# FNet mixing followed by a sigmoid GLU on one Trainium2 core: batch 1's row copies, table loads and folds moved to earlier steps

## The chip, the cores and the metric

The kernel runs on one core of a Trainium2 chip, in float32 throughout. The metric is the device time of one execution in microseconds (us), the median of the runs shown. The core has five engines with a queue of instructions each: PE (matmuls; PEld is its weight loading), DVE (vector), ACT (scalar), POOL (GpSimd) and SP (sync, which here only issues DMAs). An engine takes its instructions in program order. The data of a DMA are moved by 16 DMA engines that all issuers share.

## The reference

```python
X = np.fft.fft(x, axis=1)                  # x: (8, 3008, 256) float32
X = np.fft.fft(X, axis=2)
x = X.real.astype(np.float32).reshape(8 * 3008, 256)
gate = 1.0 / (1.0 + np.exp(-(x @ w_gate))) # (256, 1536)
val = x @ w_val                            # (256, 1536)
out = (gate * val) @ w_out                 # (1536, 256)
```

## The kernel before

**Mathematics.** The DFT over the 256 features is folded into the gate and value weights once, at the start: `merge` (L410) multiplies each block of weights by the table `dt` and leaves the cosine and sine forms in `G1` and `G2` and one row of them, by DMA, in `ge`. The DFT over the 3008 positions is done per batch. The rows of a batch are brought into an order in which symmetric rows stand beside each other, added and subtracted ("folded"), and multiplied on PE by small tables of cosines and sines. The results are `pk` and `qk`, one column per pair of output rows k and 3008 - k. One feature column (number 128) goes its own way: `x8` holds it for batches 1 to 7, `e_joint` (L731) transforms it, the row `er` is stored to `ed` in DRAM and comes back, broadcast over the partitions, as `ek`.

**Steps.** The main loop (L1143) runs over 576 steps: 8 batches, 6 chunks of at most 252 columns, 12 blocks of 128 hidden features. A batch is 72 steps (`per`), a chunk 12 (`i0`). Step i forms the gate and value sums of block i in a PSUM bank: `seed` (ACT, L767) writes `ek` times `ge` into it, `front_a` adds the part of `pk` and `front_b` that of `qk` (PE). `gate_a` and `gate_b` (ACT and DVE) turn the two output rows of each pair into gated values `h`, a step later. `back(p, part)` (L852) multiplies them by `w_out` five steps later: three blocks form group p, and step i runs `back((i - 5) // 3, (i - 5) % 3)`. From group 4 on this takes 15 products instead of 18, for which POOL prepares sums: seven (`H_SUMS[1]`) after the group's second block and six (`H_SUMS[2]`) after its third, into the tile `sf` (L819). The products of part 1 read h5, sum 13, h8, sum 11 and sum 12, in this order; sum 11 is finished by the first of the six. At a chunk's end, `finish` (L893) spreads further sums on DVE, transposes into the tile `os` and 16 stores from SP over the next steps. `os` and `er` share one buffer (pool `op`, one buffer).

**The order of the work is written by hand.** `at(i, f)` puts f at the end of step i, `gap` into the middle of `gate_b`, `spare` ahead of `gate_b`. An engine sees the instructions in exactly this order. SP does not wait for steps: it issues as soon as the waits of each DMA allow. DMAs use eight completion semaphores in turn ("lanes", of ACT's DMAs too), and a DMA waits until the one eight before it has landed.

What batch 1 needs in its preparation, with the steps of before:

- weights: `weight_load` for jobs 13 to 17 at steps 4 to 8 (512 KB each, into the buffer `x4`, which batch 1's rows take later); two tiny `ge` DMAs per merge (L420)
- `quarter_x(1)` (L150): 23 DMAs that copy batch 1's rows within DRAM, from the input into `xr` in the needed order: three small ones of zeros, two of 384 KB (L168), 18 of 124 or 128 KB (L163); at steps 9 to 14
- `load_x(1)` (L143): `xr` into SBUF, two DMAs of 1536 KB; step 14
- `table_rows` (L203): six copies of 188 KB within DRAM, into `rtab`; step 15
- `raw_tables` (step 17) and `quarter_load` (L241, steps 18 and 19): 16 loads of 141 KB into the tile `st`; `quarter_small`, `quarter_other` and `small_ops` then form a few columns of ratios from them; `ratios[6]` is the reciprocal of L278
- `e_load` (L682): the 128th column of batches 1 to 7, seven DMAs of single floats, steps 23 to 29; `e_fold` (four POOL sums) at step 38; `e_joint` at step 40
- `fold_ops(1, 2)` (L485): 24 operations on the rows: eight additions over the feature mirror on POOL (L496, L492), six `across` sums (L505; five on DVE, one on POOL), six `feat` (L499 to L502) and four half sums (L531) on POOL; steps 21 to 51
- `e_rows(i)` (L749): loads `ek` of a chunk; the one of step 36 is issued by ACT, all others by SP

Of the kernel before, what the change touches and what calls it, by code (L numbers as in the profile page):

```python
# [81 lines left out]
def kernel(  # L82
# [10 lines left out]
    nc = tc.nc  # L93
    B, _, _, _, D = xf.shape
    F = moe_w_gate.shape[1]
    P = 128
# [5 lines left out]
    NFT = F // P  # L102
# [40 lines left out]
    def load_x(b):  # L143
        X[b] = xp.tile([P, 4, NQ, D], F32, name="x4", tag="x4")
        for h in range(0, 4, 2) if b else ():
            nc.sync.dma_start(out=X[b][:, h : h + 2], in_=XR[b][:, h : h + 2])
# [3 lines left out]
    def quarter_x(b):  # L150

        copy = nc.sync.dma_start
        src = xf[b]
        dst = XR[b] = dram.tile([P, 4, NQ, D], F32, name=f"xr{b}")
        ops = [lambda: copy(out=dst[TB : TB + 1, :, N3], in_=zero[0:1].to_broadcast([1, 4, D]))]
        for q in (1, 1 + N3):
            ops.append(lambda q=q: copy(out=dst[HP - 1 : HP, :, q], in_=zero[0:1].to_broadcast([1, 4, D])))

        def run(lo, q, t, step, skip=0, less=0):
            n = TB - skip - less  # L160
            p0 = t // NQ + step * skip
            rows = src[p0 : p0 + n] if step > 0 else src[p0 - n + 1 : p0 + 1]
            copy(out=dst[lo + skip : lo + skip + n, :, q].rearrange("p h d -> h p d"),  # L163
                 in_=rows[:, :, t % NQ].rearrange("p h d -> h p d")[:, ::step])

        for par in range(2):
            lo = par * HP
            ops.append(lambda par=par, lo=lo: copy(out=dst[lo : lo + TB, :, 0:N3], in_=src[0:TB, :, par:NQ:2]))  # L168
            for q in range(N3):
                own = 2 * q + par  # L170
                less = int((par, q) == (0, 1))
                first = int((par, q) == (0, 0))
                ops += [lambda a=a: run(*a) for a in (
                    (lo, N3 + q, M // 2 - own, -1), (lo + TB, q, M // 4 - own, -1, 0, less),
                    (lo + TB, N3 + q, M // 4 + own, 1, first, less))]
        return ops
# [12 lines left out]
    ed = dram.tile([B, NK + 1], F32, name="ed")  # L189
# [13 lines left out]
    def table_rows(par, q):  # L203

        p0, qq = divmod(M // 4 - 2 * q - par, NQ)
        nc.sync.dma_start(
            out=rtab[par * TB : (par + 1) * TB, :, q].rearrange("p t k -> t p k"),
            in_=stab[p0 - TB + 1 : p0 + 1, :, qq].rearrange("p t k -> t p k")[:, ::-1])
# [29 lines left out]
    def quarter_src(g, par, t, cols):  # L238
        return (stab[0:TB, t, par:NQ:2, cols], rtab[par * TB : (par + 1) * TB, t, :, cols])[g]

    def quarter_load(t, par):  # L241


        for name, cols in (("odd", slice(NE, NE + NO)), ("ev", slice(0, NE))):
            for g, own, lo in TILES:
                if own == par:
                    nc.sync.dma_start(out=TAB[name][lo : lo + TB, t ^ g, :, 0 : cols.stop - cols.start],
                                      in_=quarter_src(g, par, t, cols))

    def quarter_small(which, part):  # L250

        for g, par, lo in TILES:
            at_ = slice(lo, lo + TB)
            if (g, par) == (which, part):
                nc.scalar.copy(TAB["self"][at_, 0:N3], TAB["ev"][at_, g, :, 0])
                nc.scalar.copy(TAB["angle"][at_].rearrange("p (t q) -> p t q", t=2),
                               TAB["odd"][at_, :, :, 0] if g == 0 else TAB["odd"][at_, ::-1, :, 0])
# [6 lines left out]
    def small_ops():  # L264

        vec, sign = nc.vector, TAB["sign"]

        def signs():
            for g, par, lo in TILES:
                nc.gpsimd.memset(sign[lo : lo + TB], (1.0, -1.0)[g])  # L270
        return signs, (
            lambda: vec.reciprocal(TAB["less"], TAB["cos"]),
            lambda: vec.tensor_tensor(TAB["tan"], TAB["sin"], TAB["less"], op=ALU.mult),
            lambda: vec.tensor_scalar(out=TAB["less"], in0=TAB["tan"], scalar1=-1.0, scalar2=None, op0=ALU.mult),
            lambda: vec.reciprocal(TAB["self"], TAB["self"]),
            lambda: vec.tensor_tensor(TAB["other"], TAB["other"], TAB["self"], op=ALU.mult),
            lambda: vec.tensor_scalar(out=TAB["other"], in0=TAB["other"], scalar1=sign, scalar2=None, op0=ALU.mult),
            lambda: vec.reciprocal(TAB["cy"], TAB["ev"][:, 0, :, 1]),  # L278
            lambda: vec.tensor_tensor(TAB["cx"], TAB["ev"][:, 1, :, 1], TAB["cy"], op=ALU.mult),
            lambda: vec.tensor_scalar(out=TAB["cx"], in0=TAB["cx"], scalar1=sign, scalar2=None, op0=ALU.mult),  # L280
            lambda: vec.tensor_scalar(out=TAB["cy"], in0=TAB["cx"], scalar1=-1.0, scalar2=None, op0=ALU.mult))
# [391 lines left out]
    def seq_start(b):  # L673
        PQE[b] = [pqp.tile([P, NK + 1], F32, name=name, tag=name) for name in ("pk", "qk")]
        for t in PQE[b]:
            nc.vector.memset(t[:, NK:], 0.0)
# [5 lines left out]
    def e_load(b):  # L682
        nc.sync.dma_start(out=x8[:, b - 1], in_=xf[b, :, :, :, HD : HD + 1])
# [57 lines left out]
    H, SF, EK = {}, {}, {}  # L741
# [7 lines left out]
    def e_rows(i):  # L749

        b, c, _ = groups[i // 3]
        k0, n = chunks[c]
        EK[i // NFT] = ekp.tile([P, CH], F32, name="ek", tag="ek")[:, 0:n]
        queue = nc.scalar if i == 3 * NFT else nc.sync
        queue.dma_start(out=EK[i // NFT], in_=ed[b : b + 1, k0 : k0 + n].to_broadcast([P, n]))

    PF, AP, Z = {}, {}, {}
    N1 = 5
# [240 lines left out]
    sin[1][1]()()  # L999
    weight_join(3)  # L1000
    e_rows(0)

    per = NFT * len(chunks)
    side, mid, gap, spare = {}, {}, {}, {}

    def at(i, *fs):
        side.setdefault(i, []).extend(fs)
# [18 lines left out]
    i0 = NFT  # L1026
    count = 3 * len(groups)
    calm = lambda lo: (i for i in range(lo, count) if 3 <= i % i0 <= 7)
    for i, f in enumerate(quarter_x(1)):
        at(i0 - 3 + i // 4, f)  # L1030
    at(i0 + 2, lambda: load_x(1))
    for b in range(1, B):
        at(22 + b, lambda b=b: e_load(b))
    at(3 * i0 + 2, e_fold)
    later_e = []
    at(3 * i0 + 4, lambda: later_e.extend(e_joint()))
    at(3 * i0 + 5, lambda: later_e[0]())
# [1 line left out]
    at(3 * i0 + 6, made_tables)  # L1039
    at(3 * i0 + 8, lambda: later_e[2]())  # L1040
    for i in range(i0, count, i0):
        if i == 3 * i0:
            spare[i - 11] = [lambda: e_rows(3 * i0)]
        else:
            at(i - (8 if i == i0 else 11), lambda i=i: e_rows(i))

    for i in range(NQ):
        at(15, lambda i=i: table_rows(i % 2, i // 2))
    at(17, raw_tables)
    for i in range(4):  # L1050
        at(18 + i // 2, lambda i=i: quarter_load(i // 2, i % 2))
    signs, ratios = small_ops()
    at(i0, signs)
    for i in range(4):
        spare.setdefault(34 + i // 2, []).append(lambda i=i: quarter_small(i // 2, i % 2))
    at(36, quarter_other)
    for i, f in zip((36, 36, 37, 42, 43, 44, 34, 35, 51, 52), ratios, strict=True):
        gap.setdefault(i, []).append(f)

    def first_folds():  # L1060

        slots = [21, 21, 21, 22, 22, 23, 24, 25, 25, 26, 27, 27, 28, 28, 30, 33, 36, 38, 40, 42, 44, 46, 48, 51]
        for i, f in zip(slots, fold_ops(1, 2), strict=True):
            at(i, f)
        for i, f in enumerate(TURN.pop(1)):
            if i in (1, 4):
                at((38, 40)[i // 4], f)
            else:
                gap[(38, 0, 39, 40, 0, 41)[i]] = [f]
        swaps, last, first = MORE.pop(1)  # L1070
        at(41, swaps[1])
        at(52, swaps[0])
        for i, f in enumerate(first):
            gap.setdefault(45 + i, []).append(f)
        for i, f in enumerate(last):
            gap[56 + i] = [f]

    def first_ends():
        one, two = quarter_ends(1, 1), quarter_ends(1, 0)
        for i, f in zip((55, 65, 65, 66, 66, 67, 67, 68, 68, 69, 69, 70, 70, 71, 71, 72, 73, 74, 75, 76),  # L1080
                        one[0] + two[0] + one[1] + two[1], strict=True):
            gap.setdefault(i, []).append(f)
    at(19, first_folds)
    at(3 * i0 + 14, lambda: seq_start(1))
    for blk in range(2):
        mid[(5 - blk) * i0 + 5] = lambda blk=blk: quarter(1, blk)
# [56 lines left out]
    for i in range(count):  # L1143
# [13 lines left out]
        n = 3 if i >= count - 8 else 2 + (i % 2 and i not in (3 * i0 + 7, 3 * i0 + 9))  # L1157
# [80 lines left out]
```

## Time and profile before

| | |
|---|---|
| median of 3 runs (lowest to highest) | 1918.88 us (1918.55 to 1919.31) |
| the profiled execution | 1919.43 us |
| its span, first to last instruction | 1917.6 us |
| PE busy | 1900.3 us, 99% |
| DVE, ACT, POOL busy | 80%, 71%, 81% |
| granted PE clock, mean | 0.998 |
| chain of work that ended last: PE | 93% |
| queue 1 of the DMAs | 195752 packets, 106.37 MB |

A step can be found in the trace by the start of its `pf<-qk` matmuls:

| step | 8 | 16 | 21 | 26 | 31 | 35 | 36 | 40 | 41 | 42 | 43 |
|---|---|---|---|---|---|---|---|---|---|---|---|
| us | 76.24 | 103.36 | 118.98 | 134.61 | 152.27 | 164.77 | 169.36 | 181.86 | 187.40 | 194.18 | 200.17 |

How to read it: "idle before" and "waits" name what an engine waited for; SPq is the queue of SP's DMA issues. The chain of work is followed back from the last instruction. In a table by stretches, each line has the length, each engine's busy time with its number of instructions, the granted PE clock (1.00 is full), the mean busy share of the 16 DMA engines and GB/s. A timeline line has start, duration, engine, line of the kernel, operation, and out<-in.

### The profile page before, as it was taken

Reading aid. Unit: us, or ns where it says so; the run is one execution under the profiler, and the core shown is the slowest. Engines: PE = TensorE matmul, PEld = TensorE weight load, DVE = VectorE, ACT = ScalarE, POOL = GpSimd, SP = SyncE. Lnnn points to the kernel's source line nnn. Section 1 sums busy time; section 2 is a strip of 40 time slices with the busy share of each in tenths; the row PEclk is TensorE's granted clock in tenths of the full one; section 3 lists DMA queues with packets and bytes.
Section 4 is the critical chain, followed back from the end, with each engine's and each line's share of the span. In section 5 each row is a group of like instructions: output and inputs, shape, how many; then the busy total and the mean of one; then the engine's idle time right before and its main releaser. Section 6 shows DMA issues by size and latency. Waiting matters only on the chain.

```text
span 1917.6 us, 36046 instructions
## 1 busy us (share of the span) xinstructions
PE 1900.3 (99%) x11836; PEld 1758.3 (92%) x11836; DVE 1526.9 (80%) x3368; ACT 1353.5 (71%) x3235; POOL 1545.6 (81%) x2733
## 2 busy tenths in 40 slices
PE   8999999999999999999999999999999999999999
PEld 5788899999999999999999999999999999999998
DVE  7677888787978789797788877888788887977775
ACT  4876777777677777777777777677777777777775
POOL 2488879986999779997799877999789986877770
PEclk9999999999999999999999999999999999999999
DMA  8336331212022121221212112112120110010001
GB/s 313 96 124 77 89 105 44 66 46 81 15 52 72 31 80 24 63 52 32 87 36 57 42 37 86 39 47 51 33 80 15 34 41 15 15 23 19 15 18 30
DMA packets 196661, 109.33 MB, mean 57 GB/s; under 512 B 134791, under 2 KB 187762, under 8 KB 194682
## 3 DMA queue, kind: packets, MB, share of 16 engines
q1 hardware_dynamic: 195752, 106.37, 20.9%
q8 instruction: 95, 1.56, 0.4%
q14 instruction: 92, 0.75, 0.1%
q10 hardware_dynamic: 690, 0.64, 0.1%
q0 software_dynamic: 32, 0.00, 0.0%
HBM read 71.24 MB, written 47.87 MB: 62 GB/s over the span
## 4 chain that ended last, share of the span: by engine, by line
PE 93%; DMA 2%; DVE 1%; POOL 1%; ACT 1%; SPq 1%; issue 0%; DVEq 0%; ACTq 0%; POOLq 0%
PE pf L133 49%; PE po L133 41%; PE sum L133 2%; DMA x<-in_xf_dram 1%; POOL sf L819 1%; DMA rtab<-in_stab_dram 1%; PE ps L133 1%; DMA st<-rtab 1%; DMA raw<-in_moe_w_val_dram 0%; DVE z L797 0%; PE ev L133 0%; SPq L926 0%; PE od L133 0%; POOL x L505 0%; ACT pf L767 0%
## 5 line engine op out<-in xcount | busy, mean ns | idle before, releaser
L819 POOL TENSOR_TENSOR sf<-h,sf 128x168 f32<-128x168 f32 (+1 forms) x1104 | 619.6, 581 | 78.9 <-DVE h L813 76.9
L819 POOL TENSOR_TENSOR sf<-h 128x168 f32<-128x168 f32 (+1 forms) x920 | 521.7, 586 | 167.4 <-DVE h L813 166.3
L133 PE MATMUL pf<-qk,G 128*128 128x252 f32 (+1 forms) x2304 | 585.2, 377 | 4.7 <-ACT ae L782 4.5
L133 PE MATMUL pf<-pk,G 128*128 128x252 f32 (+1 forms) x2304 | 583.9, 376 | 1.2 <-ACT pf L767 1.2
L767 ACT ACTIVATE pf<-ek,ge 128x252 f32<-128x252 f32 (+1 forms) x1142 | 538.5, 471 | 22.3 <-DVE h L813 2.6
L133 PE MATMUL po<-sf,wf 128*128 128x168 f32 (+1 forms) x2944 | 509.3, 306 | 0.0
L782 ACT ACTIVATE ae<-pf 128x504 f32<-128x504 f32 (+1 forms) x576 | 339.2, 589 | 211.7 <-PE pf L133 210.4
L133 PEld LDWEIGHTS pf<-pk,G 128*128 128x128 f32 x2304 | 435.9, 190 | 55.8 <-ACT pf L767 3.6
L133 PEld LDWEIGHTS po<-sf,wf 128*128 128x128 f32 x2944 | 454.5, 190 | 8.1
L133 PE MATMUL po<-h,wf 128*128 128x168 f32 (+2 forms) x2584 | 461.2, 307 | 0.0
L813 DVE TENSOR_TENSOR h<-pf,z 128x252 f32<-128x252 f32 (+1 forms) x576 | 240.7, 418 | 267.0 <-ACT pf L810 263.0
L797 DVE TENSOR_TENSOR z<-ae,pf 128x504 f32<-128x504 f32 (+1 forms) x576 | 385.0, 668 | 83.6 <-ACT h L796 80.0
L903 DVE TENSOR_TENSOR c<-c 128x168 f32<-128x168 f32 (+1 forms) x920 | 443.5, 505 | 3.3
L133 PEld LDWEIGHTS pf<-qk,G 128*128 128x128 f32 x2304 | 410.7, 190 | 37.9 <-ACT ae L782 7.3
L133 PEld LDWEIGHTS po<-h,wf 128*128 128x128 f32 x2584 | 410.3, 190 | 17.6 <-issue 0.9
L796 ACT ACTIVATE h<-pf 128x252 f32<-128x252 f32 (+1 forms) x576 | 217.3, 377 | 144.9 <-PE pf L133 130.8
L810 ACT ACTIVATE pf<-z 128x252 f32<-128x252 f32 (+1 forms) x576 | 214.5, 372 | 133.4 <-DVE h L809 130.9
L809 DVE TENSOR_TENSOR h<-h,pf 128x252 f32<-128x252 f32 (+1 forms) x576 | 233.3, 405 | 0.0
L819 POOL TENSOR_TENSOR sf<-sf 128x168 f32<-128x168 f32 (+1 forms) x184 | 102.0, 554 | 14.4
L819 POOL TENSOR_TENSOR sf<-sf,h 128x168 f32<-128x168 f32 (+1 forms) x184 | 111.1, 604 | 0.0
L886 ACT COPY c<-po 128x504 f32<-128x504 f32 (+1 forms) x138 | 78.6, 570 | 0.0
L913 DVE STREAM_TRANSPOSE os<-c 128x256 f32<-128x256 f32 x188 | 76.6, 428 | 0.1
(151 smaller groups left out, 878.8 us busy)
## 6 DMA issues: line engine op xcount, KB each, us to landing
x<-xr SPq DMA_DIRECT2D x14, 1536.0 KB
out_dram<-os SPq DMA_DIRECT2D x376, 56.0 KB
xr<-in_xf_dram SPq DMA_DIRECT2D x105, 128.0 KB
x<-x SPq DMA_DIRECT2D x112, 96.0 KB
xr<-in_xf_dram SPq DMA_DIRECT2D x14, 384.0 KB
ek<-ed SPq DMA_DIRECT2D x39, 126.0 KB
out_dram<-os SPq DMA_DIRECT2D x288, 7.0 KB
x<-in_xf_dram SPq DMA_DIRECT2D x3, 1024.0 KB
```

The lines of the kernel that those rows point to most:

```text
L133: nc.tensor.matmul(o, l, r, start=start, stop=stop, skip_group_check=True)
L767: nc.scalar.activation(PF[i][:, g], EK[i // NFT], AF.Copy, scale=ge[:, g, f : f + 1])
L782: nc.scalar.activation(AP[i], PF[i], AF.Copy, scale=2.0)
L796: nc.scalar.activation(H[p][:, fh, 0:n], PF[i][:, 0], AF.Sigmoid)
L797: nc.vector.tensor_tensor(z[:, :, ::-1], AP.pop(i), PF[i], op=ALU.subtract)
L809: nc.vector.tensor_tensor(h[:, fh, 0:n], h[:, fh, 0:n], pf[:, 1], op=ALU.mult)
L810: nc.scalar.activation(pf[:, 0], z[:, 0], AF.Sigmoid)
L813: nc.vector.tensor_tensor(h[:, fh, n:], pf[:, 0], z[:, 1], op=ALU.mult)
L819: nc.gpsimd.tensor_tensor(block(p, dst), block(p, a), block(p, b), op=(ALU.subtract, ALU.add)[op])
L886: (nc.vector.tensor_copy if t == 1 or t == 3 else nc.scalar.copy)(C[0][:, 3 * t * R : 3 * (t + 1) * R], PO[t][:, 0 : 3 * R])
L903: nc.vector.tensor_tensor(t[:, dst * R : (dst + 1) * R], *v, op=(ALU.subtract, ALU.add)[op])
L913: nc.vector.transpose(os_[0][0][:, s, 0:nb, h, :], t[:, c0 : c0 + nb * TB])
```

## The change

Nothing that is computed changes; only when and by whom it is issued. `quarter_x(1)` moves from steps 9 to 14 to steps 1 to 10: two DMAs a step beside the weights, then four and three. `table_rows` moves from step 15 to steps 11 and 12, which puts it ahead of `load_x(1)`, now at step 13 (it was behind it). `raw_tables`, `quarter_load` and `e_load` move four steps ahead, `quarter_small` and the ratios three to seven, `e_fold` two. The folds run from step 17 to 50 instead of 21 to 51. The chunk's `ek` of step 36 is issued by SP at step 25 instead of ACT at step 25.

```diff
-        queue = nc.scalar if i == 3 * NFT else nc.sync
-        queue.dma_start(out=EK[i // NFT], in_=ed[...].to_broadcast([P, n]))
+        nc.sync.dma_start(out=EK[i // NFT], in_=ed[...].to_broadcast([P, n]))
...
     for i, f in enumerate(quarter_x(1)):
-        at(i0 - 3 + i // 4, f)
-    at(i0 + 2, lambda: load_x(1))
+        at(1 + i // 2 if i < 16 else 9 + (i - 16) // 4, f)
+    at(i0 + 1, lambda: load_x(1))
     for b in range(1, B):
-        at(22 + b, lambda b=b: e_load(b))
-    at(3 * i0 + 2, e_fold)
+        at(18 + b, lambda b=b: e_load(b))
+    at(3 * i0, e_fold)
...
     for i in range(i0, count, i0):
-        if i == 3 * i0:
-            spare[i - 11] = [lambda: e_rows(3 * i0)]
-        else:
-            at(i - (8 if i == i0 else 11), lambda i=i: e_rows(i))
+        at(i - (8 if i == i0 else 11), lambda i=i: e_rows(i))
 
     for i in range(NQ):
-        at(15, lambda i=i: table_rows(i % 2, i // 2))
-    at(17, raw_tables)
+        at(11 + i // 3, lambda i=i: table_rows(i % 2, i // 2))
+    at(i0 + 1, raw_tables)
     for i in range(4):
-        at(18 + i // 2, lambda i=i: quarter_load(i // 2, i % 2))
+        at(14 + i // 2, lambda i=i: quarter_load(i // 2, i % 2))
...
-        spare.setdefault(34 + i // 2, []).append(lambda i=i: quarter_small(i // 2, i % 2))
-    at(36, quarter_other)
-    for i, f in zip((36, 36, 37, 42, 43, 44, 34, 35, 51, 52), ratios, strict=True):
+        spare.setdefault(27 + i, []).append(lambda i=i: quarter_small(i // 2, i % 2))
+    at(31, quarter_other)
+    for i, f in zip((32, 33, 34, 42, 43, 44, 30, 31, 51, 52), ratios, strict=True):
         gap.setdefault(i, []).append(f)
...
-        slots = [21, 21, 21, 22, 22, 23, 24, 25, 25, 26, 27, 27, 28, 28, 30, 33, 36, 38, 40, 42, 44, 46, 48, 51]
+        slots = [17, 17, 17, 18, 19, 20, 21, 22, 23, 24, 25, 25, 26, 26, 28, 30, 33, 35, 37, 39, 41, 44, 47, 50]
         for i, f in zip(slots, fold_ops(1, 2), strict=True):
             at(i, f)
         for i, f in enumerate(TURN.pop(1)):
-            if i in (1, 4):
-                at((38, 40)[i // 4], f)
-            else:
-                gap[(38, 0, 39, 40, 0, 41)[i]] = [f]
+            gap[35 + i] = [f]
...
-    at(19, first_folds)
+    at(16, first_folds)
```

## The prediction

> **What bounds the kernel now.** I read the page first, then the table by stretches, the waits, the chain of waits and, where something stalls, the timeline and the semaphore records.
>
> ```profile
> PE 1900.3 (99%) x11836; PEld 1758.3 (92%) x11836; DVE 1526.9 (80%) x3368; ACT 1353.5 (71%) x3235; POOL 1545.6 (81%) x2733
> ```
>
> PE is busy 99% of the span, and the change removes no matmul. A step takes 3.12 us of PE time (3.39 in the first chunk), so the change can win or lose only where PE stops, is slow, or where its clock is low. Two stretches show that:
>
> ```profile
> 161.64:169.36 7.72, 6.52 (x39) 5.81 (x38) 3.31 (x12) 5.34 (x19) 5.98 (x12) 1.00 1.13 65
> 187.40:200.17 12.77, 9.28 (x38) 8.18 (x37) 8.70 (x23) 5.51 (x13) 6.67 (x13) 0.73 0.58 136
> ```
>
> The first is steps 34 and 35: 7.72 us instead of 6.25, so 1.47 lost. The second is steps 41 and 42: 12.77 instead of 6.25, so 6.52 lost; PE is busy 9.28 us of it and the clock's mean is 0.73. The waits say who was late:
>
> ```profile
> DVE er L711 <- DMA xr<-zero: 5.6, 1, 5.6
> PE pf L133 <- ACT ae L782: 4.3, 3, 3.5
> DVE small L278 <- DMA st<-rtab: 3.9, 1, 3.9
> ```
>
> DVE stood 3.9 us for the tables of `quarter_load` and 5.6 us to clear `er`, which shares its buffer with `os` and so waits for the stores of `os`. The chain shows why both came late:
>
> ```profile
> 131.25 3.03 DMA ek<-ed
> ...
> 135.51 13.08 DMA rtab<-in_stab_dram
> ...
> 159.52 5.88 DMA st<-rtab
> ...
> 165.43 0.07 DVE small L278
> ```
>
> SP's queue stood 15.8 us (its own waits) until ACT had issued `ek` at 131.25, since that DMA has a lane which the fourth `rtab` copy needs; then `rtab`, 16 table loads, seven `e_load` (to 179 us) and only then the stores, the last landing at 189.30. PE waited 3.49 us in step 42, its clock was halved from 193.0 to 199.8, and step 42 took 5.99 us.
>
> **The change, part by part.**
>
> *The stalls that go.* `ek` of step 36 is no longer in ACT's queue, so SP doesn't stand for it; the table loads end near 138 (below) and L278, now in step 30, comes near 160 (149.0 and the delay below): -1.47. The `e_load` DMAs end (below) near 155, so the stores of `os` are out before step 41: -6.52 with the clock's part. Behind this stall nothing is late: without 5.6 us DVE would have been ready for step 42 by 188.6, before PE reaches it at 190.5. At steps 48 to 51 0.57 us are lost beside a full POOL, which gets one fold less there: I take -0.2 (0 to -0.57).
>
> *The `across` sums.* Steps 26 to 30 lose 2.05 us. There DVE runs five L505 that take 2.89, 1.70, 0.68, 0.91 and 1.06 us, against 0.69 early in the kernel with POOL idle. They move to steps 23 to 26 and POOL is as full there: 0 gained (0 to -2.05).
>
> *Copies beside the weights.* A copy of 128 KB has four parts; one after the other they land 1.35 us apart. A weight takes 1.36 us on 16 engines, a 384 KB copy 1.05. Parts are served in order (shown below), so from step 4 on the engines of the copies have two copies and a weight to do in 5.12 us, 4.1 us, and from step 8 on 3.4 us per step. Weights of jobs 14 to 17 land by 68.5, 72.9, 77.3 and 82.6, and ACT wants them at 70.0, 74.7, 79.8 and 83.2: hidden. The `ge` of step 6 lands at 71.3 instead of 69.2; ACT's seed of step 8 waits 2.1 us longer, but PE wants it at 71.97: hidden. If that cover were gone, some 2 us would go there, and be taken off the wait that follows.
>
> *Table copies ahead of the rows.* Here I see the cost. How `rtab` runs:
>
> ```profile
> 122.00:132.00 10.00, 10.00 (x59) 9.41 (x59) 4.68 (x11) 7.05 (x17) 9.92 (x16) 1.00 0.13 50
> ```
>
> A share of 0.13 of 16 is two engines. The six copies landed at 125.41, 129.31, 133.25, 140.73, 144.65 and 148.60: 3.92 us each, one after another, though 14 engines were free. And what is issued behind them waits on those two: the first store of `os`, issued at 136.19, had 14 of its 16 parts landed by 138.4 and the last two at 148.7 and 148.8, behind the sixth `rtab`. So parts are served in order on each engine. In the changed order on SP, all six stand ahead of the two halves of `load_x(1)`. From the issue times and services above: the 23rd row copy lands near 94.8 (a chain of 19 lost 1.3 us to hiccups before; I take 1 us), six times 3.92 gives 118.3, and two parts of `x` at 3.65 to 4 each give 122.2 and T = 126.2, though 14 of 16 parts are there by 105. That assumes that the two engines of `rtab` are among the four of the copies. I take it because short DMAs never spread to free engines in this trace. If not, `rtab` starts at 87.3, ends at 110.8, and T = 118.1. The ends for T are 118.1 and 128.
>
> The Trainium skill, "DMA: Bandwidth & Descriptors", section on why a DMA increments its semaphore by 16, states that a DMA from SP runs on the lowest-numbered k of the 16 engines, k being the largest number up to 16 that divides the slowest dimension of both sides; here that would be 2 for `rtab` and 4 for the copies. By it the first of the two sums holds and the second is out; the share of 0.13 agrees with k = 2, and no run here shows which two.
>
> Before, POOL found the rows at 123.47, landed since 121.83. Now it comes to the first fold after the seven sums of group 5:
>
> ```profile
> 110.36 0.53 POOL L819 TENSOR_TENSOR sf<-h 128x168 f32<-128x168 f32 x1
> 111.42 1.64 POOL L819 TENSOR_TENSOR sf<-h,sf 128x168 f32<-128x168 f32 x3 [0.53 <-DVE h L813]
> 118.41 0.73 PE L133 MATMUL po<-sf,wf 128*128 128x168 f32 x4
> ```
>
> It reaches the fold at 110.9 and stands until T. Behind the folds of step 17 in its queue are the six sums of group 5, first sum 11. PE reads it at 118.41 (step 21, part 1). After T come L496 (0.2 us), L492 (1.25) and one sum (0.6): T + 2.1 = 128.3. PE waits 128.3 - 118.4 = **9.9 us** (1.8 to 11.7). What is late before step 21 is absorbed here.
>
> *After the wait.* POOL is 15 us behind: six sums to T + 4.8, two folds to T + 7.3, seven sums to T + 11.4, a fold, sum 11 of group 6 at T + 13.2. PE at full speed would be there at T + 2.1 + 9.4 = T + 11.5: at least 1.7 us more. But PE is not at full speed: after 3.49 us without matmuls the clock was halved for 6.83 us, 5.65 of them after PE went on, which cost step 42 2.87 us. All four clock changes of the trace are multiples of 3.41 us apart, a grid, so the time at half clock after PE resumes depends on where in it that falls: 3 to 6.8 us, costing 1.5 to 3.4. It covers POOL's 1.7. I take **+2.4** (1.7 to 3.4). Group 7 is due at T + 23.2, ready at T + 22.9 or a little later; I add nothing.
>
> *What else is issued.* On SP behind `load_x`: `ek` of step 24 lands with T, used by step 23, after the wait. The 16 table loads, 0.7 us each behind T, end near 138; ACT reads them at step 27, about 149. Stores of chunk 0 to 142, `e_load` at 2 us each to 156, `ek` of step 36 near 158, wanted at about 175. All hidden, by the wait itself.
>
> **Sum** against the profiled execution: 9.9 + 2.4 - 1.5 - 6.5 - 0.2 = +4.1 us, 1921.7 of span. The profiled execution was 1919.43, 0.55 above the median; on the median it gives 1918.88 + 4.1 = **1923.0 us**.
>
> **The rivals.**
>
> *The rows come in time* (faster; the way in which the forecast's wait isn't there). If the parts of `x` overtake `rtab` on the shared engines, or take turns with it, T is near 111, POOL waits for nothing, and 8.2 us go: 1910.7. If they only queue behind `rtab` on engines that the copies don't use, T = 118.1: PE waits 1.8, then 2 us for POOL's backlog, 1914.5. For it: 14 of 16 engines are free. Against it: the store whose two parts waited 10 us. 17%.
>
> *Half the wait* (no change). If `rtab` starts between the copies, or two engines alone move `x` faster, T = 122: PE waits 5.7 us and the sum is zero, 1919. Against it: 3.92 us for each `rtab` with no other load. 10%.
>
> *The clock stays low* (slower still). The wait is three times that of step 42 and spans whole steps of the grid; if the clock then needs two grid steps more to return, another 6.83 us at half speed cost 3.4: 1926.4. It decides from the moment that PE's pause covers two grid steps, 6.8 us. Against it: at step 42 one stretch was enough. 13%.
>
> The Trainium skill, "TensorE: Matmul & The Clock Gate", part 1, tells of a free-running window of 3413 ns, after one idle one of which the clock is halved and after one busy one is full. By this the low clock after the wait lasts at most two windows, and this rival falls; the grid of the trace agrees, and no run yet shows a pause of 10 us.
>
> **How the numbers follow.** Forecast 60%, its own range 1920 to 1926.5 (T within 2 us, the clock's 1.7 to 3.4). Two measurements of this kernel can be told apart from 0.2%, 3.8 us: the bounds are 1915.0 and 1922.7. Slower: 34 of the forecast's 60, all 13 of the clock: 47%. Same: 26 and 10: 36%. Faster: 17%. The range leaves out most of the rows in time (17%, down to 1910.7) and little above the third rival: 1914 to 1929.
>
> **What would show it.** Right: POOL idle some 15 us ahead of L496, ended by DMA `x<-xr`, near 126; PE idle near 10 us in step 21, ended by POOL; a low clock after it; no wait of DVE at L278 or L711; steps 34, 35, 41 and 42 at 3.12 (step 40 keeps 2.4 us of `pe` matmuls). Wrong: L496 at 111 without a wait, or `x` landed while `rtab` is still on its way; then the time is below 1915. A pause of ACT at L382 or of PE ahead of step 16 would say that the copies do hold up the weights, which I cost at nothing.

## The result and the profile after

The changed kernel takes **1926.32 us** (median of 5 runs, 1925.52 to 1927.31); the kernel before, measured beside it, 1918.55 (1918.35 to 1919.31). The ratio is 1.004, with a 95% interval of 1.0025 to 1.0055: slower by 0.4%. The forecast was 1923.0. In the profiled executions the span grew from 1917.6 to 1924.5 us, by 6.9, where the sum had 4.1.

The line numbers of the changed kernel are one lower from `e_rows` on: `seed` is L766, the sums into `sf` are L818, the clearing of `er` is L710. A step is measured from the start of its `pf<-qk` matmuls to that of the next step, so PE's wait at 118 us of the kernel before lies at the end of step 20.

First the table by stretches of the changed kernel (length; busy time and number of instructions of PE, PEld, DVE, ACT, POOL; granted clock; DMA share; GB/s). Its lines are steps 7 to 10, step 20, step 21, step 35, steps 41 and 42, and steps 47 and 48:

```profile
70.85:89.32 18.47, 16.12 (x57) 10.31 (x55) 9.37 (x20) 13.84 (x36) 4.92 (x5) 1.00 0.47 150
118.89:131.95 13.06, 4.00 (x21) 3.56 (x19) 3.02 (x9) 2.65 (x7) 3.46 (x7) 0.69 0.46 118
131.95:136.18 4.23, 4.23 (x19) 3.75 (x19) 1.01 (x2) 1.57 (x4) 4.15 (x7) 0.74 0.88 218
178.16:181.28 3.12, 3.12 (x20) 2.94 (x19) 3.12 (x9) 2.12 (x6) 3.04 (x7) 1.00 0.07 15
199.32:205.57 6.25, 6.25 (x38) 5.89 (x37) 5.90 (x13) 5.02 (x12) 6.25 (x11) 1.00 0.41 102
218.08:226.22 8.14, 6.77 (x39) 5.69 (x37) 6.07 (x14) 4.51 (x12) 7.54 (x14) 1.00 0.01 2
```

The same steps of the kernel before, for the first and the last of these lines:

```profile
71.12:86.41 15.29, 15.29 (x58) 10.74 (x57) 9.23 (x20) 13.11 (x34) 5.53 (x6) 1.00 0.43 125
212.67:219.02 6.35, 6.35 (x38) 5.80 (x36) 6.33 (x14) 4.04 (x11) 6.27 (x12) 1.00 0.01 3
```

Step 35 takes 3.12 us and steps 41 and 42 take 6.25, PE busy throughout: the two stalls of the kernel before are gone. Step 20 takes 13.06 us with PE busy for 4.00 of them, and step 21 is slow with a busy PE at a clock of 0.74. And the first line, which the forecast had at no loss, has 2.35 us without matmuls, and the last line has 1.37. The waits say why, first from 60 to 100 us, then from 100 to 240 us:

```profile
ACT pf L766 <- DMA ge<-G: 7.1, 3, 4.1
```

```profile
POOL x L496 <- DMA x<-xr: 14.6, 2, 11.0
...
PE po L133 <- POOL sf L818: 9.9, 2, 9.1
...
ACT st L318 <- POOL st L295: 2.0, 1, 2.0
```

The second fence's first two lines are the forecast's wait: POOL stands for the rows, PE for POOL. DVE's waits at L278 and for `er` do not appear any more. The other two lines, ACT's wait for `ge` and ACT's wait for a small POOL operation, were 1.1 and 0.6 us in the kernel before. The chain of waits (start, length, what) shows two of the three in their places:

```profile
67.00 5.61 DMA ge<-G
...
78.53 4.12 DMA ge<-G
...
104.62 20.17 DMA x<-xr
...
130.12 2.48 POOL sf L818 x5
```

The same trace against the kernel before, by stretches, in us gained (-) or lost (+); the numbers are differences of step starts:

| steps | forecast | measured |
|---|---|---|
| start to 7 | 0 | -0.27 |
| 7 to 11 | 0 | +3.31 |
| 20 and 21 (wait, then clock and backlog) | +12.3 | +11.04 |
| 26 to 30 (`across`) | 0 | -0.68 |
| 35 | -1.47 | -1.47 |
| 41 and 42 | -6.52 | -6.52 |
| 47 to 50 | -0.2 | +1.79 |
| all later | 0 | -0.27 |
| sum | +4.1 | +6.9 |

### The profile page after: what moved, and what is told of

It reads as the page before. It is cut to its first block, busy times and chain, and to the rows that moved or that the text cites. A ratio compares the mean times of both kernels' runs of the same rounds, so it can differ in the third digit from the quotient of the medians.

```text
span 1924.5 us, 36049 instructions
## 1 busy us (share of the span) xinstructions
PE 1900.8 (99%) x11836; PEld 1758.3 (91%) x11836; DVE 1520.1 (79%) x3368; ACT 1351.8 (70%) x3235; POOL 1542.9 (80%) x2733
## 4 chain that ended last, share of the span: by engine, by line
PE 87%; POOL 5%; DMA 3%; DVE 2%; ACT 2%; issue 1%; SPq 0%; POOLq 0%; ACTq 0%; DVEq 0%
PE pf L133 46%; PE po L133 38%; POOL sf L818 3%; PE sum L133 2%; DMA x<-xr 1%; POOL x L492 1%; DMA x<-in_xf_dram 1%; DMA ge<-G 1%; DVE c L902 1%; DVE z L796 0%; POOL x L505 0%; PE ps L133 0%; ACT pf L766 0%; DMA raw<-in_moe_w_val_dram 0%; DVE h L812 0%
## 5 line engine op out<-in xcount | busy, mean ns | idle before, releaser
L818 POOL TENSOR_TENSOR sf<-h,sf 128x168 f32<-128x168 f32 (+1 forms) x1104 | 619.5, 581 | 77.8 <-DVE h L812 75.4
L818 POOL TENSOR_TENSOR sf<-h 128x168 f32<-128x168 f32 (+1 forms) x920 | 520.7, 585 | 160.5 <-DVE h L812 159.4
L766 ACT ACTIVATE pf<-ek,ge 128x252 f32<-128x252 f32 (+1 forms) x1142 | 538.2, 471 | 27.0 <-DMA ge<-G 7.1
L808 DVE TENSOR_TENSOR h<-h,pf 128x252 f32<-128x252 f32 (+1 forms) x576 | 232.8, 404 | 0.0
L818 POOL TENSOR_TENSOR sf<-sf 128x168 f32<-128x168 f32 (+1 forms) x184 | 101.9, 554 | 14.4
L818 POOL TENSOR_TENSOR sf<-sf,h 128x168 f32<-128x168 f32 (+1 forms) x184 | 109.6, 595 | 0.0
```

Of the source, the lines that this page charges most:

```text
L766: nc.scalar.activation(PF[i][:, g], EK[i // NFT], AF.Copy, scale=ge[:, g, f : f + 1])
L808: nc.vector.tensor_tensor(h[:, fh, 0:n], h[:, fh, 0:n], pf[:, 1], op=ALU.mult)
L818: nc.gpsimd.tensor_tensor(block(p, dst), block(p, a), block(p, b), op=(ALU.subtract, ALU.add)[op])
```

## The experiments

The theory after the result: the mechanism of the forecast is right (the stalls at 35, 41 and 42 go; the table copies ahead of the rows cost a wait of PE with a slow clock behind it), and the missing 2.8 us come from two things costed at nothing, the row copies beside the weights and a fold that was moved in front of L295. The rivals: that the order of the table copies and the rows doesn't matter and the rows are late for another reason; and that the stalls went for another reason than `ek` of step 36.

| kernel | us, median | ratio to before, 95% interval | span of the profile |
|---|---|---|---|
| changed | 1926.32 | 1.0025 to 1.0055 | 1924.5 |
| e1_ek_on_sp | 1916.64 | 0.9984 to 1.0003 | 1914.0 |
| e2_rows_first | 1913.76 | 0.9966 to 0.9985 | 1912.1 |
| e3_rows_on_act | 1913.74 | 0.9965 to 0.9984 | 1912.8 |
| e4_feat_slots | 1924.84 | 1.002 to 1.0046 | 1921.9 |
| e5_ge_on_act | 1919.86 | 0.9997 to 1.0016 | 1917.8 |
| e6_front_undone | 1930.84 | 1.0045 to 1.0075 | 1928.8 |
| e7_ge_and_feats | 1919.51 | 0.9996 to 1.0015 | 1916.7 |
| e8_copies_sparse | 1913.86 | 0.997 to 0.999 | 1912.1 |
| e9_folds_from_20 | 1913.04 | 0.9964 to 0.9984 | 1913.4 |
| e10_all_in_time | 1908.47 | 0.9936 to 0.9964 | 1906.6 |

The kernel before took 1918.5, 1918.58, 1918.1 and 1918.02 us beside e1 to e4, e5 to e7, e8 and e9, and e10. Differences of one or two us are read from the steps, not from these medians.

**e1: one part alone, `ek` of step 36 on SP.** The kernel before, with

```diff
-        queue = nc.scalar if i == 3 * NFT else nc.sync
-        queue.dma_start(
+        nc.sync.dma_start(
```

> The kernel before, with one line changed: SP issues the ek of step 36, not ACT. Theory (SP stood 15.8 us for a lane that ACT had not yet used, and everything behind slipped): SP's wait goes, the table loads land near 150 and the e_load DMAs end some 10 us sooner; DVE waits neither at L278 nor ahead of clearing er; steps 35, 41 and 42 lose nothing: -8.0 us, near 1910.5. Rival (these stalls come from the steps at which loads are issued, so the new slots are needed for the gain): at most step 35's 1.5 us go, 1917 to 1918.5.

Measured: steps 41 and 42 win their 6.52 us, so SP's stand behind ACT's `ek` was the cause of the late stores. But step 35 takes 6.48 us and step 36 3.67: 2.44 us more are lost there than in the kernel before. SP now issues this `ek` behind two `e_load` at 160.70, it lands at 166.00, and ACT stands for it; PE stands 1.96 us behind that, and its clock is halved from 168.30 to 171.72 (waits from 150 to 240 us):

```profile
ACT pf L766 <- DMA ek<-ed: 2.6, 1, 2.6
```

Steps 46 to 50 lose 1.43 us more. So this part of the change brings its gain of 6.52 by itself, and the rest of the gain is not there while the other loads stay late.

**e2: the table copies behind the rows.** The changed kernel, with

```diff
-        at(11 + i // 3, lambda i=i: table_rows(i % 2, i // 2))
+        at(i0 + 1 + i // 3, lambda i=i: table_rows(i % 2, i // 2))
```

> The changed kernel, but the six rtab copies are issued at steps 13 and 14, behind the two row loads of step 13. Theory (the rows waited in order behind rtab on two DMA engines): rows landed by 106, POOL does not wait at L496, PE does not wait at step 21 and its clock stays full: the 11.0 us of steps 20 and 21 go, the late ge of steps 7 to 9 (3.3 us) and step 47 (1.8) stay, and the across sums may take back 0.7: near 1916. Rival (POOL is overfull once folds start at step 17): POOL still finishes sum 11 of group 5 late and PE still waits several us between steps 20 and 26: above 1920.

Measured: the rows land at 102.30 and 106.03 instead of 124.78 and 128.63, POOL doesn't wait for them, the clock stays full, and the 11.04 us of steps 20 and 21 shrink to 0.29. This is one line of the diff, and it decides the sign of the whole change. Steps 20 and 21 in the table by stretches:

```profile
118.94:122.22 3.28, 3.28 (x18) 2.87 (x18) 2.83 (x5) 1.99 (x6) 3.28 (x5) 1.00 0.26 87
122.22:125.47 3.25, 3.25 (x19) 2.96 (x19) 2.80 (x7) 2.16 (x6) 3.25 (x6) 1.00 0.15 54
```

Three losses stay: 2.83 us in steps 7 to 11, which therefore do not come from the table copies, 1.37 us in steps 19 to 23, which the wait had covered, and 0.60 us of the 1.79 in steps 46 to 50.

**e3: the rows on another queue, the order kept.** The changed kernel, with the two halves of `load_x(1)` issued by ACT:

```diff
-            nc.sync.dma_start(out=X[b][:, h : h + 2], in_=XR[b][:, h : h + 2])
+            (nc.scalar if b == 1 else nc.sync).dma_start(out=X[b][:, h : h + 2], in_=XR[b][:, h : h + 2])
```

> The changed kernel, but the two row loads of step 13 are issued by ACT, so they go to another queue of the same 16 DMA engines; rtab stays ahead of them in time. Theory (order holds within one queue, and the engine takes turns between two): the last parts of the rows land near 112 to 119 instead of 128.6; PE waits 0 to 2 us at step 21; 1916 to 1918. Rival (the engines themselves are taken, whichever queue asks): rows land after the sixth rtab, 128 or later, and the time stays near 1926.

Measured: the rows land at 104.74 and 109.43, while the six table copies, ahead of them in the program, land from 99.15 to 126.61. Of these, SP had begun to issue four before ACT issued the first rows at 95.50; three of the four, from the second (110.78) on, land after the rows. So it is the order within SP's queue that holds the rows back, not the two engines as such: the rows of another queue pass table copies that were issued before them. That removes the first rival.

**e4: the last `feat` folds back to steps 46, 48 and 51.** The changed kernel, with

```diff
-        slots = [..., 35, 37, 39, 41, 44, 47, 50]
+        slots = [..., 35, 37, 39, 41, 46, 48, 51]
```

> The changed kernel, with the last three feat folds at steps 46, 48 and 51 as before instead of 44, 47 and 50. Theory (a feat of 1.8 us put ahead of the table sum L295 in POOL's queue made ACT's L318 wait 2.0 us in step 47): ACT does not wait there, steps 47 and 48 take 3.1 and 3.2 to 3.3 us, -1.8 us, near 1924.5. Rival (the step 47 loss comes from POOL's backlog of the late rows): the same 1926.3, and L318 still waits.

Measured: steps 47 to 50 lose 0.20 us instead of 1.79. In the changed kernel POOL does the fold of step 44 (L499 to L502, 214.48 to 216.44), then six sums, and reaches L295 at 220.14; ACT scales its result in L318. ACT at that place (start, duration, engine, line, operation, what ended the idle time):

```profile
217.85 0.98 ACT L766 ACTIVATE pf<-ek,ge 128x252 f32<-128x252 f32 x2
220.86 0.68 ACT L318 ACTIVATE st<-st 128x570 f32<-128x570 f32 x1 [2.03 <-POOL st L295]
```

The engine that waits is ACT, 2.03 us, and the work of PE behind it is late. The fold is not the whole cause: with the fold at step 44 too, but the rows in time, e2 loses only 0.60 us in these steps.

**e5: `ge` on another queue.** e2_rows_first, with the `ge` DMAs of `merge` issued by ACT:

```diff
-            nc.sync.dma_start(
+            nc.scalar.dma_start(
                 out=ge[:, g, f : f + 1], in_=G2[0:1, g, f * P : (f + 1) * P])
```

> The changed kernel with the table copies behind the rows (as in e2_rows_first), and in addition the tiny ge DMAs (L420) issued by ACT instead of SP. Theory A: in steps 7 to 11 the ge of steps 6 and 8 land 4.5 and 3.7 us after their issue instead of 1.45, because they stand on SP's queue behind parts of row copies; on another queue they land in about 1.5 us, steps 7 and 9 are 5.1 and 3.4 us long as in the kernel before, and the 2.4 to 3.3 us come back: span 1909 to 1910 against 1912.1 of e2_rows_first. Theory B: the ge also wait for the engine itself, whoever issues them, so their landing stays at 3.5 to 5 us and nothing changes: 1912. Theory C: ACT's DMA has a lane that the copy eight DMAs before it still holds, ACT stands for it ahead of its seeds, and steps 4 to 12 grow by 2 us or more: 1914 or above.

Measured: theory A fell. The `ge` still land 2.2 to 4.8 us after the end of their issue (at 66.93, 71.62 and 77.68), nearer to theory B. Of the one issued at 77.68, 12 of 16 parts landed by 79.94 and the last four at 82.78 to 82.90, behind a weight and a row copy that SP had issued at 76.07 and 76.53, and ahead of a row copy issued at 77.19: on another queue it passed one copy, not what stood before that. And the time went up by 5.6 us of span against e2, as theory C said, though for a nearer reason than a lane: ACT spends 1.13 us on the issue of each pair, between the copies of `G` and the `h` that DVE waits for. ACT's timeline:

```profile
66.80 0.38 ACT L418 COPY G<-ps 128x256 f32<-128x256 f32 x1
66.93 1.13 ACTq L420 DMA_DIRECT2D ge<-G  x2
68.11 0.38 ACT L795 ACTIVATE h<-pf 128x252 f32<-128x252 f32 x1 [0.93 <-ACT G L418]
```

Steps 0 to 6, where ACT stands four times 0.93 us like this, lose 3.36 us; steps 7 to 11 lose 4.08 instead of 2.83.

**e6: the early half undone.** The changed kernel, with copies, rows, table copies and first folds where they were before:

```diff
-        at(1 + i // 2 if i < 16 else 9 + (i - 16) // 4, f)
-    at(i0 + 1, lambda: load_x(1))
+        at(i0 - 3 + i // 4, f)
+    at(i0 + 2, lambda: load_x(1))
...
-        at(11 + i // 3, lambda i=i: table_rows(i % 2, i // 2))
-    at(i0 + 1, raw_tables)
+        at(15, lambda i=i: table_rows(i % 2, i // 2))
+    at(16, raw_tables)
...
-        at(14 + i // 2, lambda i=i: quarter_load(i // 2, i % 2))
+        at(17 + i // 2, lambda i=i: quarter_load(i // 2, i % 2))
```

(and the list of fold steps and the `TURN` loop of the kernel before).

> The changed kernel with its early half undone: row copies, load_x, table copies (behind load_x) and the first folds at the steps of the kernel before; what stays of the change is the later half (raw tables and table loads one step sooner in the program, e_load and e_fold, ratios, ek of step 36 on SP). Theory A, the forecast's terms: the late half alone is worth steps 35, 41 and 42, -8.0 us, and the early half alone costs. Steps 7 to 11 as before (5.12, 4.5, 3.39), no wait at L496, step 21 at 3.1; steps 26 to 30 keep their 2.05; span near 1909.6 if the table loads are out in time. Theory B: as in e1_ek_on_sp, ek of step 36 or the table loads come late again behind the stores, so that 3 to 4 of the 8 us come back at steps 35, 36 and 46 to 48: 1913 to 1914. Which of the two is read at steps 35 to 48.

Measured: neither theory. Steps 7 to 11, 35, 41 and 42 are as theory A said, but step 27 takes 21.21 us. PE's wait and its releaser, from 90 to 240 us:

```profile
PE pf L133 <- ACT ae L781: 18.7, 4, 17.9
...
ACT small L255 <- DMA st<-in_stab_dram: 15.2, 1, 15.2
```

`quarter_small`, which the change has in step 27 instead of 34, stands in ACT's queue for table loads that SP issues only from 149.08 on, behind six table copies (to 145.55) and 16 stores. As it is written, the later half of the change can't be had without the earlier: each consumer that moves ahead needs its loads moved with it. Steps 46 to 50 lose 1.49 us, with the folds at their old steps, much as in e1 (1.43). The run also gives the longest pause of PE: 17.93 us. The halved clock then lasted from 145.10 to 162.17, 17.07 us, which is five times 3.413; PE was back at 158.91, so 3.3 us of it fell on matmuls.

**e7: e5 and e4 together.**

```diff
-        slots = [..., 35, 37, 39, 41, 44, 47, 50]
+        slots = [..., 35, 37, 39, 41, 46, 48, 51]
```

> e5_ge_on_act with the last three feat folds at steps 46, 48 and 51 (as in e4_feat_slots). Theory: the two parts add up, steps 47 and 48 lose nothing (3.12 and 3.4 or less), 0.5 to 0.8 us below e5_ge_on_act: 1908.5 to 1909.5 of span if theory A of that run holds. Rival: the folds only meet another of POOL's sums (steps 46 or 49 grow by as much) and the time is that of e5_ge_on_act.

Measured: steps 46 to 50 are 0.98 us shorter than in e5 (-0.36 against the kernel before, +0.62 in e5), step 35 is 0.30 longer; the spans differ by 1.1. The effect of the folds adds up; the base, as seen, was a bad one.

**e8: fewer copies ahead of `ge`.** The change with e2's and e4's edits, and

```diff
-        at(1 + i // 2 if i < 16 else 9 + (i - 16) // 4, f)
+        at((1, 1, 2, 2, 3, 3, 4, 5, 6, 8, 8, 8, 8, 9, 9, 9, 9, 10, 10, 10, 10, 11, 11)[i], f)
```

> The changed kernel with the table copies behind the rows (e2_rows_first), the last feat folds at 46, 48 and 51 (e4_feat_slots), and the row copies thinned out while the last ge DMAs are issued: two a step in steps 1 to 3, one in steps 4, 5 and 6, none in 7, then four, four, four and two at the ends of steps 8 to 11. Theory: the ge DMAs of steps 6 and 8 landed late because two and more copies stood ahead of them on their engine; with fewer they land about 1.5 to 2.5 us after issue, and steps 7 and 9 are 5.1 to 5.4 and 3.4 to 3.7 us: of the 2.8 us lost there in e2_rows_first at least 2 come back. The rows land some 3 us later, near 109, still before POOL asks for them. With 0.7 us of steps 47 to 49: 1908.5 to 1909.5 of span. Rival 1: the weights of 512 KB alone delay the ge, and steps 7 to 11 stay 2 us or more too long: 1911.5. Rival 2: the rows land after POOL's first fold and the wait at step 20 returns: 1914 or above.

Measured: the `ge` of step 6 lands 1.79 us after the end of its issue instead of 4.53 in e2, that of step 8 1.44, and steps 7 to 11 lose nothing (0.00 against 2.83). So the loss was the row copies, and not the weights. Steps 19 to 23 lose 0.05 instead of 1.37; one of DVE's sums for the `wf` tables is held up there (1.50 us at 117.58) where e2 has three, and PE, ACT and DVE come to these steps less late. Which of the two counts is not shown. But the span is that of e2: the rows land at 107.29 and 111.58, the table copies behind them 4.5 us later than in e2, the table loads at 146.13, and ACT waits in step 27, then in step 35. From 130 to 182 us:

```profile
ACT small L256 <- DMA st<-in_stab_dram: 3.3, 1, 3.3
...
ACT pf L766 <- DMA ek<-ed: 1.5, 1, 1.5
```

The steps were as the theory had them, the span was not: against e2, 5.2 us came off in steps 7 to 11, 19 to 23 and 46 to 50, and 5.2 were lost in steps 27, 28 and 35.

**e9: the folds from step 20.** As e8, with

```diff
-        slots = [17, 17, 17, 18, 19, 20, 21, 22, 23, 24, 25, 25, 26, 26, 28, 30, 33, 35, 37, 39, 41, 46, 48, 51]
+        slots = [20, 20, 20, 21, 21, 22, 22, 23, 24, 25, 25, 26, 26, 27, 28, 30, 33, 35, 37, 39, 41, 46, 48, 51]
...
-    at(16, first_folds)
+    at(18, first_folds)
```

> e8_copies_sparse with the folds of batch 1 begun at step 20 instead of 17 (three at 20, then 21, 21, 22, 22, 23 for the point folds, 24 to 27 for the across sums). In e2_rows_first three of DVE's sums for the wf tables (L453, L456) took 1.53, 1.35 and 1.35 us, where they take 0.41, 0.63 and 0.28 in the kernel before, each beside the start of one of POOL's large folds (L492), and steps 19 to 23 lost 1.4 us. Theory: DVE is held while POOL runs such a fold, so most of this loss goes, since DVE's wf sums end in step 22; but POOL has more folds in steps 24 to 27, and if DVE's across sums meet point folds there again, steps 25 to 28 lose part of it: 0 to 1.2 us below e8_copies_sparse. Rival: the loss moves whole to steps 24 to 30, as in the kernel before (2.05 us there): equal or up to 1 us above e8_copies_sparse.

Measured: inconclusive for its question, since e8 had already lost only 0.05 us in steps 19 to 23, and waits for loads in steps 27 and 35 (2.7 us for `ek`) cover what follows. The medians differ by 0.8 us one way, the spans by 1.3 the other: the profiled execution, 1915.19 us, is the longest of e9's eight, and the others took 1912.76 to 1913.27.

**e10: everything in time.** As e8, with

```diff
-        spare.setdefault(27 + i, []).append(lambda i=i: quarter_small(i // 2, i % 2))
+        spare.setdefault(30 + i // 2, []).append(lambda i=i: quarter_small(i // 2, i % 2))
...
-        at(18 + b, lambda b=b: e_load(b))
+        at(25 + b, lambda b=b: e_load(b))
```

> e8_copies_sparse with two further moves: quarter_small at steps 30 and 31 instead of 27 to 30, and the seven e_load at steps 26 to 32 instead of 19 to 25, behind the ek of step 36. In e8_copies_sparse ACT stood 3.3 us in step 27 for the table loads (ended 146.1) and 1.5 us in step 35 for that ek (issued behind the seven e_load, landed 167.5), and steps 27, 28 and 35 lost 5.2 us. Theory: nothing else is late there, so the 5.2 us come off: steps 27, 28 and 35 at 3.12, span near 1907, time near 1908.5. Rival: e_load now ends near 168 and POOL's e_fold, at the end of step 36, waits for it with the sums behind it, so that steps 37 and 38 lose 1 to 3 us: 1908 to 1910 of span.

Measured: 1908.47 us (1908.37 to 1909.07, 5 runs), 0.5% below the kernel before, and the span of the theory. Steps 7 to 10, 20 and 21, 26 to 30, 35, 41 and 42, 47 and 48 in the table by stretches of this kernel:

```profile
70.90:86.19 15.29, 15.29 (x58) 10.74 (x56) 9.23 (x20) 13.29 (x34) 5.58 (x6) 1.00 0.45 146
115.64:121.88 6.24, 6.24 (x38) 5.88 (x37) 5.34 (x10) 3.87 (x10) 6.16 (x10) 1.00 0.14 52
134.39:150.01 15.62, 15.62 (x92) 14.72 (x91) 12.70 (x27) 12.62 (x33) 15.38 (x30) 1.00 0.71 151
162.51:165.63 3.12, 3.12 (x20) 2.94 (x19) 3.07 (x9) 2.18 (x6) 2.96 (x6) 1.00 0.58 9
183.68:189.93 6.25, 6.25 (x38) 5.89 (x37) 5.69 (x13) 5.03 (x12) 6.25 (x11) 1.00 0.57 139
202.43:208.68 6.25, 6.25 (x38) 5.89 (x37) 6.24 (x14) 4.34 (x11) 6.17 (x11) 1.00 0.01 3
```

In each line PE's busy time is the whole stretch. The rival (a wait for `e_load` at steps 37 and 38) did not come. Of the 11.0 us, 6.52 are steps 41 and 42, 2.04 the `across` steps, 1.47 step 35.

## Why the prediction was right, and where its sizes were off

The sum's large terms were right by their mechanism; two small ones were wrong, the copies beside the weights (0) and steps 47 to 50 (-0.2).

*The stalls that go* (-1.47 and -6.52): both to the hundredth. The table loads ended at 138.67 (forecast 138), the stores of chunk 0 at 143.4, the last `e_load` at 159.6 (156), `ek` of step 36 at 161.6 (158). e1 shows that the 6.52 hang on who issues that `ek`. The prediction's list of what came behind SP's stand in the kernel before is short of one item: 16 stores of chunk 0, issued from 136.19 to 152.08, stood between the table copies and the table loads.

*Table copies ahead of the rows*: T was 128.63 (forecast 126.2, ends 118.1 to 128, so just past the upper end). Of the 2.4 us, 1.6 are the last row copy (96.43 instead of 94.8), 0.6 the second half of the rows (3.85 us behind the first, which itself landed 4.63 behind the sixth table copy: 8.5 for both, forecast 7.9), 0.2 the table copies (23.7 us from the last row copy to the sixth, forecast 23.5). The first table copy landed 3.52 us after the last row copy, its two parts 3.93 us after the first two of that copy's four (96.00 and 96.01): it stood behind it, as the first of the two sums assumed. e2 and e3 show the cause from two sides. PE went on at 130.67, T + 2.04 (forecast T + 2.1), after a wait of 9.06 (9.9).

*After the wait*: the 13.06 and 4.23 us of steps 20 and 21 are 11.04 too many; less the wait of 9.06 this leaves 1.98 for clock and backlog, against 2.4 (1.7 to 3.4). The clock was halved from 123.94 to 134.18, 10.24 us, three times 3.413; PE used 3.5 us of it: it was back just before the last of the three grid steps. In the Trainium skill, "TensorE: Matmul & The Clock Gate", part 1, the window is 3413 ns and one busy window is enough; the trace agrees, and so does e6 with five windows and 3.3 us of matmuls at half clock after a pause of 17.93. For the halving the prediction took over one idle window; less was enough in these runs: e1's pause of 1.96 us, inside the grid step that ends at 168.30, was followed by half a clock. The rival of a clock that stays low is out, although the measured time, 1926.32, is nearly the 1926.4 that it gave: the right number for another reason.

*Copies beside the weights* (costed at 0, "hidden"): this is the step that failed. The forecast had the `ge` of step 6 land at 71.3 and ACT's `seed` wait 2.1 us longer, with PE wanting it later. It landed at 72.61, ACT stood 4.11 us, the `ge` of step 8 came as late once more (2.28), and steps 7 to 11 lost 3.31 us. I had put two copies and a weight per step against the length of the step, so an average, where the queue of one engine counts: at 67.00 it held parts of two copies and of a weight. Of this `ge`, 12 of 16 parts landed by 68.91, and the last four, from 71.06 to 72.61, behind the four parts of the second copy (70.87 to 72.32). e8 takes those copies away, and the loss is gone. The sign that the prediction named for this, a pause of PE ahead of step 16, came, but through `ge` and not through the weights. The forecast also said that such a loss "be taken off the wait that follows". That was right, and so the 3.31 us did not cost 3.31: PE came to the wait 3.2 us later and waited less. What they and the copies did cost is T, 2.4 us later than forecast. The late row copies follow from the same wait by the order in the trace: SP issued nothing from 70.66 to 74.91, until ACT had copied the `G` that the next `ge` reads, and the copies behind it came from 76.78 on. No run isolates this.

*Steps 47 to 50* (costed at -0.2): +1.79. I counted that POOL gets one fold less in steps 48 to 51, and not that the fold of step 46, moved to 44, then stands in front of L295 in POOL's queue, for which ACT waits. e4 shows that the fold matters. But so does how late POOL is: L295 starts 2.06 us after the start of step 47 in the changed kernel, 0.85 in e2 (same folds, rows in time, 0.60 lost), 1.21 in e1 and e6 (folds at their old steps, 1.43 and 1.49 lost) and 0.06 in the kernel before. That in e1 and e6 POOL misses the stall of steps 41 and 42, in which it could catch up, is argued.

*The `across` sums* (0, to -2.05): -0.68. They took 0.71, 0.68, 1.91 (two of them) and 0.75 us where the first two had taken 2.89 and 1.70; step 26 alone lost more than before (4.48 us instead of 3.33). In e10 steps 26 to 30 lose nothing, the full 2.05.

Together: T +2.4, steps 47 to 50 +2.0, clock and backlog -0.4, `across` -0.7, start and later steps -0.5: the 2.8 us between 4.1 and 6.9.

What stays open: why step 26 of the changed kernel takes 4.48 us and that of e4 3.74; both lie behind the wait, with POOL catching up, and no run takes that apart. And how much of the 0.8 us between e8 and e9 is real.

## What to carry to other kernels

When a DMA is issued sooner, list what it then stands ahead of, in its issuer's queue and on each of the engines that it uses, down to the tiniest transfer: here six copies turned a gain into a loss by standing in front of rows that were wanted some 40 us before them, and a few copies in front of a row of 512 bytes cost 3 us. Count such a queue at the moment of the issue, not as an average over a step. And move a consumer only as far ahead as its loads move, since on a hand-ordered engine one early reader (e6, e8) stops everything behind it.

## What the runs showed of the hardware that I had not expected

- Order holds within a queue, not between queues: the rows issued by SP behind the table copies landed at 128.63; issued by ACT at the same place they landed at 109.43, while those copies ran to 126.61. But the tiny `ge` gained little from another queue: it landed 2.2 to 4.8 us after the end of its issue in e5, against 1.44 in e8 with no row copy ahead of it.
- Two small DMAs issued by ACT took 1.13 us there, and ACT's next instruction stood 0.93 us for them (e5).
- PE's clock was halved after pauses shorter than a step of the grid (3.413 us): after 1.96 us in e1 and 2.10 us in e8. A pause of 2.26 us in e9 (to 142.95), which the grid, counted back from the change at 169.17, cuts in two at 141.86, was not followed by a halving.
- Some sums of DVE that meet one of POOL's large folds last as long as that fold. In e2_rows_first DVE's L453 started at 113.91 and took 1.53 us (0.41 in the kernel before); it ended at 115.44, and POOL's L492 ran from 113.89 to 115.15:

```profile
113.91 1.53 DVE L453 TENSOR_TENSOR wf<-wc 128x256 f32<-128x256 f32 x1
```

```profile
113.89 1.26 POOL L492 TENSOR_TENSOR x<-x 128x510 f32<-128x510 f32 x1
```

Two more pairs of the same trace look alike (L456, 1.35 us each, which ended 0.15 us after their folds). Not every operation is held: L808, which reads `pf` from PSUM, took its usual 0.40 us at 120.57, inside the fold from 119.87 to 121.18. No run isolates what decides.
